# A place's mix weights issued ahead of its share of the weights' conversion, and two conversion steps moved

## The chip, the cores and the metric

The kernel runs on one core of a Trainium2 chip. A core has five engines that run side by side, each through its own instructions in order: TensorE (matrix products; PE in the profile, its weight loads PEld), VectorE (DVE), ScalarE (ACT), GpSimd (POOL) and SyncE (SP, which only issues DMAs here). They wait for each other through semaphores. The metric is the device time of one execution in microseconds (us).

## The reference

Attention with the heads mixed before and after the softmax, then a gated two-layer network without bias:

```python
# q, k, v: (8, 12, 448, 64); w_pre, w_post: (12, 12); w_in: (768, 2048); w_out: (2048, 768)
scores = np.matmul(q, k.transpose(0, 1, 3, 2)) / np.sqrt(64)
scores = np.einsum('bhij,hg->bgij', scores, w_pre)
scores = scores - np.max(scores, axis=-1, keepdims=True)
attn = np.exp(scores)
attn = attn / (np.sum(attn, axis=-1, keepdims=True) + 1e-09)
attn = np.einsum('bhij,hg->bgij', attn, w_post)
x = np.matmul(attn, v)                  # heads put side by side: (3584, 768)
h = x @ w_in
out = (h - np.tanh(h)) @ w_out          # (3584, 768), float32
```

`w_in` and `w_out` arrive as 64-bit floats. The chip computes in 32 bits, so the kernel converts them itself.

## The kernel before, in words

There are two stages. In the first (to about 848 us of the span) the kernel computes the attention, one batch after another, and beside it converts the weights. In the second it runs the network in blocks of 512 rows.

**Places.** The attention goes through 180 places, `for p in range(NPL + 3)` at L1255. One place handles two groups of ten tokens each, all twelve heads of a group lying across the partitions. The loop body gives every engine its instructions of this place, and each engine keeps the order in which they were issued (`in_order`, L134). Before the change a place `p` issues, in this order:

1. `mixed()`: ScalarE copies the result of the last mix out of PSUM (L966, or L973 in two pieces).
2. `conv.place()`: this place's share of the weights' conversion (below), in places 5 to 180.
3. SP's DMAs: `gather` brings the scores of later groups (L906), `issue(6)` sends up to six waiting loads and stores (L765).
4. `premix(p)`: TensorE multiplies the gathered scores by `w_pre` into two PSUM banks `ps_p` (L917). The pool has just these two banks, so the next premix needs both to have been read.
5. `norm(p - 1)`: VectorE adds 1e-9 to the sums `zs` of the exponentials of the place before (L937, twice) and takes the reciprocal (L938); GpSimd multiplies `w_post` by it into `wr` (L939). This folds the softmax's division into the mix weights.
6. `expo(p)`: for each of the two banks VectorE takes the maximum (L926), and ScalarE the exponential with its sum (L928).
7. Jobs planned ahead for this place: scores of a head pair (L873), transposes of q or k (L839, L813), or a half of the values (L998); and the copies that take their results out of PSUM (L878, L824, L825, L852, L854, L1016).
8. `mix(p - 1)`: TensorE multiplies the exponentials of the place before by `wr` (L956).

Places differ in length: 64 of them hold values, and the others one or two head pairs of scores or a transpose.

**The conversion.** 48 quads of four 128 x 128 blocks are converted. `Convert.place` (L50) advances every quad under way by one step a place and starts a new one when it is due, at the earliest three places after the last; at most two are in their earlier steps. `narrow_quad` (L72) is a generator with seven steps:

1. VectorE: clamp the upper word (L81), shift the lower word (L82).
2. GpSimd: scale the upper word (L84). ScalarE: scale the lower word (L85).
3. VectorE: sign (L90), join (L91), exponent (L94).
4. GpSimd: multiply and add (L96, L97); the result is `m`.
5. ScalarE: rounded copy of `m` (L100). GpSimd: four sums of the blocks (`sums_in` L112 or `sums_out` L123), which the second stage's seven-product scheme needs.
6. GpSimd: the remainder of `m` (L103). In `w_out`'s quads ScalarE flips the sign of one sum (L131). GpSimd: rounded copy of the sums, their high part (L105). A DMA of the converted words is put in the slow queue.
7. GpSimd: the remainder of the sums (L108). A DMA of the sums is put in the slow queue.

Of the kernel before, what the change touches and what calls it, by code (L numbers as in the profile page):

```python
# [11 lines left out]
F32R = mybir.dt.float32r  # L12
# [3 lines left out]
ALU = mybir.AluOpType  # L16
# [5 lines left out]
def raw(ap):  # L22

    return ap.bitcast(F32)
# [47 lines left out]
def narrow_quad(nc, pool, dma, r, dst, sums, sums_dst):  # L72

    p = r.shape[0]
    hi, lo = r[:, :, :, 1], r[:, :, :, 0]
    u, w = hi, lo


    lim = 122879.9921875
    m = pool.tile([p, 4, 128], F32, name="cm", tag="cm", bufs=2)  # L80
    nc.vector.tensor_scalar(m, hi.bitcast(F32), lim, -lim, op0=ALU.min, op1=ALU.max)  # L81
    nc.vector.tensor_scalar(w, lo, 8, None, op0=ALU.logical_shift_right)  # L82
    yield
    nc.gpsimd.tensor_scalar(m, m, 2.0**-112, None, op0=ALU.mult)  # L84
    nc.scalar.mul(w.bitcast(F32), w, 2.0**-44)  # L85
    yield
    o = pool.tile([p, 4, 2, 128], F32R, name="co", tag="co", bufs=2)
    oh, ol = o[:, :, 0], o[:, :, 1]
    s = ol.bitcast(I32)
    nc.vector.tensor_scalar(s, hi, -(2**31), None, op0=ALU.bitwise_and)  # L90
    nc.vector.scalar_tensor_tensor(  # L91
        out=u, in0=m.bitcast(I32), scalar=3, in1=s, op0=ALU.logical_shift_left, op1=ALU.bitwise_or
    )
    nc.vector.tensor_scalar(s, u, -(2**23), None, op0=ALU.bitwise_and)  # L94
    yield
    nc.gpsimd.tensor_tensor(out=m, in0=w.bitcast(F32), in1=s.bitcast(F32), op=ALU.mult)  # L96
    nc.gpsimd.tensor_tensor(out=m, in0=m, in1=u.bitcast(F32), op=ALU.add)  # L97
    yield
    t = pool.tile([p, 4, 2, 128], F32, name="ct", tag="ct", bufs=2)
    nc.scalar.copy(oh, m)  # L100
    done = sums(nc, m, t[:, :, 1])
    yield
    nc.gpsimd.tensor_sub(ol, m, raw(oh))  # L103
    done()
    nc.gpsimd.tensor_copy(t[:, :, 0].bitcast(F32R), t[:, :, 1])  # L105
    dma(dst, raw(o).rearrange("p x t n -> p x (t n)"))
    yield
    nc.gpsimd.tensor_sub(t[:, :, 1].bitcast(F32R), t[:, :, 1], t[:, :, 0])  # L108
    dma(sums_dst, t.rearrange("p s t n -> p s (t n)"))

# [40 lines left out]
def kernel_body(  # L151
# [11 lines left out]
    nc = tc.nc  # L163
# [72 lines left out]
    def open_ps_h():  # L236
        ff.ps_h = ctx.enter_context(tc.tile_pool(name="ps_h", bufs=2, space=PSUM, side="left"))
# [497 lines left out]
    with ExitStack() as st:  # L735
# [32 lines left out]
        def issue(most):  # L768
            for x in (queue, slow):
                while x and most and x[0][0] < place[0]:  # L770
                    send(x, nc.sync)
                    most -= 1
# [130 lines left out]
        def gather(t, eng=nc.sync):  # L903
            i, g = groups[t]
            x = tq[t % RT]
            eng.dma_start(x[D - HP : D - HP + rows[t], :], sts[i][tokens[t].start : tokens[t].stop : tokens[t].step])  # L906
            tg[t] = x

        def premix(p):


            pss = [ps_p.tile([P, S], F32, name="ps_p", tag="ps_p") for _ in halves]
            ts = [tg.pop(2 * p + j) for j in range(2)]
            for j in (1, 0):
                for r in (1, 0):
                    k = slice(r * D, D + r * H * half_rows(2 * p + j)[r])
                    nc.tensor.matmul(pss[r][halves[j], :], wpre[k, :], ts[j][k, :], start=True, stop=True)  # L917
            return pss

        def expo(p, pss):  # L920
            zs = gp.tile([P, 3, 2], F32, name="zs", tag="zs")
            es = []
            for r, ps in enumerate(pss):

                mx = gp.tile([P, 1], F32, name="mx", tag="mx")
                nc.vector.tensor_reduce(out=mx, in_=ps, axis=AX.X, op=ALU.max, negate=True)  # L926
                e = gp.tile([P, S], F32, name="e", tag="e", bufs=4)
                nc.scalar.activation(e, ps, AF.Exp, bias=mx, scale=1.0, accum_out=zs[:, 0, r : r + 1])  # L928
                es.append(e)
            te[p] = [es, zs]  # L930

        def norm(p):
            zs = te[p][1]
            wr = gp.tile([P, 2, D], F32, name="wr", tag="wr", bufs=2)[:, :, :HP]
            for r in range(2):

                nc.vector.tensor_scalar_add(zs[:, 1, r : r + 1], zs[:, 0, r : r + 1], 1e-9)  # L937
            nc.vector.reciprocal(zs[:, 2], zs[:, 1])  # L938
            nc.gpsimd.tensor_mul(  # L939
                wr, wpost[:, :HP].unsqueeze(1).to_broadcast([P, 2, HP]), zs[:, 2].unsqueeze(2).to_broadcast([P, 2, HP])  # L940
            )
            te[p].append(wr)

        def mix(p):

            es, _, wr = te.pop(p)
            ps = ps_o.tile([P, 2, 512], F32, name="ps_o", tag="ps_o")
            for j in range(2):
                i, g = groups[2 * p + j]
                if g == 0:  # L950
                    ats[i] = kp.tile([CP, NC, H, MT], F32, name="at", tag="at", bufs=2)
            for r, e in enumerate(es):
                for c in range(NC):
                    for j, a in enumerate(halves):
                        k = slice(a.start, a.start + H * half_rows(2 * p + j)[r])
                        nc.tensor.matmul(  # L956
                            ps[:CP, j, c * GP : (c + 1) * GP].rearrange("p (h i) -> p h i", i=GI)[:, :, r * GH : (r + 1) * GH],
                            e[k, c * CP : (c + 1) * CP], wr[k, r, :],
                            start=True, stop=True,
                        )  # L960

            def rest():
                (i0, _), (i1, _) = groups[2 * p], groups[2 * p + 1]
                n0, n1, at = rows[2 * p] // H, rows[2 * p + 1] // H, at_of[2 * p]
                if i0 == i1 and n0 == n1 == GI:
                    nc.scalar.copy(  # L966
                        ats[i0][:, :, :, at : at + 2 * GI].rearrange("p c h (j i) -> p j (c h) i", j=2),
                        ps[:CP, :, : NC * GP].rearrange("p j (x i) -> p j x i", i=GI),
                    )
                    return  # L970
                for j, (i, n) in enumerate(((i0, n0), (i1, n1))):
                    at = at_of[2 * p + j]
                    nc.scalar.copy(  # L973
                        ats[i][:, :, :, at : at + n],
                        ps[:CP, j, : NC * GP].rearrange("p (c h i) -> p c h i", c=NC, i=GI)[:, :, :, :n],
                    )

            return rest
# [161 lines left out]
        NPL = NG // 2  # L1140
# [23 lines left out]
        at_s, p, kind = {}, 0, None  # L1164
# [35 lines left out]
        for i, (b, m) in enumerate(blocks):  # L1200
            p0 = first[i] // 2
            if i + 2 < len(blocks):
                p = at_s[i + 2, 0] - 1
# [7 lines left out]
        for b in range(1, B):  # L1211
            p, o, done = first[blocks.index((b - 1, 1))] // 2 - 4, 0, []
            for hq in range(3):
                if hq == 2:

                    p = max(p, done[0] + 1)
# [38 lines left out]
        for p in range(NPL + 3):  # L1255
            if mixed:
                mixed()
                mixed = None
            if 5 <= p < NPL + 1:
                conv.place()  # L1260
            place[0] += 1
            for t in (2 * p + 4, 2 * p + 5):
                if t < NG:
                    gather(t)
            issue(6)
            if p == NPL + 1:
                for f in start.pop(p):
                    f()
            if p < NPL:
                ps = premix(p)  # L1270
            if 1 <= p < NPL + 1:
                norm(p - 1)
            if p == NPL:
                for f in x0[1:]:
                    f()
            if p < NPL:
                expo(p, ps)
            for f, *a in todo[p]:
                f(*a)
            for f in sooner:  # L1280
                f()
            sooner.clear()
            if 1 <= p < NPL + 1:
                mixed = mix(p - 1)
            for f in then + last:
                f()
            then.clear()
            last.clear()
            if p == NPL - 3:
                conv.rest(now)  # L1290
                early.close()
                open_early()
            if p == NPL - 1:
                early_ps.close()
                open_ps_h()
            for f in start.get(p, ()):
                f()
            for _ in range(pieces.get(p, 0)):
                next(xl)
# [88 lines left out]
```

## Time and profile before

| | |
|---|---|
| median of 3 runs | 1738.76 us (1728.68 to 1739.03) |
| profiled execution | 1736.07 us, span 1734.3 us |
| granted TensorE clock | 0.988 |
| busy: PE, PEld | 1670.9 us (96%), 1388.2 us (80%) |
| busy: DVE, ACT, POOL | 1233.1 us (71%), 1090.7 us (63%), 585.2 us (34%) |
| GpSimd idle ahead of L105, for ScalarE's L131 | 57.9 us |
| GpSimd idle ahead of L939, for VectorE's L938 | 186.6 us |

A line of the profile names engine, line and tile (out<-in); "idle before" is the time in which that engine did nothing ahead of the instruction, and the releaser is what ended the wait. A busy TensorE is not one at its peak, since matmuls are pipelined and their ends are modelled. The idle time of an engine costs nothing unless a later one waits for it.

### The profile page before, as it was taken

Reading aid. Unit: us, or ns where it says so; the run is one execution under the profiler, and the core shown is the slowest. Engines: PE = TensorE matmul, PEld = TensorE weight load, DVE = VectorE, ACT = ScalarE, POOL = GpSimd, SP = SyncE. Lnnn points to the kernel's source line nnn. Section 1 sums busy time; section 2 is a strip of 40 time slices with the busy share of each in tenths; the row PEclk is TensorE's granted clock in tenths of the full one; section 3 lists DMA queues with packets and bytes.
Section 4 is the critical chain, followed back from the end, with each engine's and each line's share of the span. In section 5 each row is a group of like instructions: output and inputs, shape, how many; then the busy total and the mean of one; then the engine's idle time right before and its main releaser. Section 6 shows DMA issues by size and latency. Waiting matters only on the chain.

```text
span 1734.3 us, 41218 instructions
## 1 busy us (share of the span) xinstructions
PE 1670.9 (96%) x16068; PEld 1388.2 (80%) x16068; DVE 1233.1 (71%) x2119; ACT 1090.7 (63%) x1920; POOL 585.2 (34%) x798
## 2 busy tenths in 40 slices
PE   8999999999999999999998999899998899999999
PEld 6776777777777677677787778788887788989999
DVE  5776777878777777775497999568776868788432
ACT  4766677777677777776486767356665365666331
POOL 1466567666666666661100111101101101101100
PEclk9999999999999999999999999999999999999999
DMA  8778889898987979865778889889889889988993
GB/s 177 218 222 246 249 235 276 248 267 255 257 253 234 259 248 257 256 203 163 249 267 282 293 286 332 306 272 347 317 309 369 298 261 346 302 316 328 402 414 139
DMA packets 322290, 475.09 MB, mean 274 GB/s; under 512 B 105264, under 2 KB 255280, under 8 KB 322096
## 3 DMA queue, kind: packets, MB, share of 16 engines
q1 hardware_dynamic: 305660, 414.34, 74.4%
q0 software_dynamic: 16128, 57.68, 8.7%
q8 instruction: 128, 2.10, 0.5%
q14 instruction: 66, 0.54, 0.1%
q10 hardware_dynamic: 308, 0.43, 0.1%
HBM read 274.73 MB, written 120.59 MB: 228 GB/s over the span
## 4 chain that ended last, share of the span: by engine, by line
PE 67%; DVE 10%; DMA 8%; issue 5%; ACT 5%; POOL 4%; SPq 1%; DVEq 0%; ACTq 0%; POOLq 0%
PE ps_o L956 11%; PE ps_m L998 6%; PE ps_p L917 6%; PE ps_h L290 6%; PE y L533 6%; PE y L531 6%; PE ps_h L291 6%; PE y L532 6%; PE ps_h L293 6%; PE ps_q L873 4%; DMA t<-s 2%; DMA vr<-in_v_dram 1%; ACT e L928 1%; DVE qa L319 1%; DMA gl<-gs 1%
## 5 line engine op out<-in xcount | busy, mean ns | idle before, releaser
L956 PEld LDWEIGHTS ps_o<-wr,e 60*112 60x112 f32 (+1 forms) x5760 | 304.6, 175 | 46.2 <-POOL wr L939 31.8
L956 PE MATMUL ps_o<-wr,e 60*112 60x60 f32 (+1 forms) x5760 | 315.6, 259 | 16.5 <-POOL wr L939 15.3
L928 ACT ACTIVATE e<-ps_p,mx 128x448 f32<-128x448 f32 x360 | 224.7, 630 | 115.1 <-DVE mx L926 83.1
L926 DVE TENSOR_REDUCE mx<-ps_p 128x1 f32<-128x448 f32 x360 | 206.5, 615 | 108.3 <-PE ps_p L917 107.7
L966 ACT COPY at<-ps_o 112x960 f32<-112x960 f32 x156 | 154.4, 989 | 109.1 <-PE ps_o L956 108.7
L917 PE MATMUL ps_p<-t,wpre 60*64 60x448 f32 (+1 forms) x1440 | 182.6, 571 | 5.9 <-DMA t<-s 5.7
L998 PEld LDWEIGHTS ps_m<-at,vr 112*64 112x64 f32 x3072 | 150.0, 138 | 26.6 <-ACT at L973 8.6
L998 PE MATMUL ps_m<-at,vr 112*64 112x120 f32 (+1 forms) x3072 | 164.2, 264 | 2.9 <-DMA vr<-in_v_dram 2.8
L531 PE MATMUL y<-w,gh 128*128 128x384 f32 x448 | 152.5, 340 | 8.0 <-DMA w<-ts 5.6
L533 PE MATMUL y<-w,gl 128*128 128x384 f32 x424 | 144.7, 341 | 7.3 <-DVE gl L449 7.3
L939 POOL TENSOR_TENSOR wr<-wpost,zs 128x120 f32<-128x120 f32 x180 | 70.0, 389 | 241.9 <-DVE zs L938 186.6
L532 PE MATMUL y<-w,gh 128*128 128x384 f32 x448 | 151.4, 338 | 0.0
L873 PEld LDWEIGHTS ps_q<-kk,qh 64*120 64x120 f32 (+1 forms) x768 | 58.8, 173 | 82.1 <-issue 45.8
L873 PE MATMUL ps_q<-kk,qh 64*120 64x448 f32 (+1 forms) x768 | 121.3, 392 | 1.1 <-DVE kk L825 0.5
L878 DVE COPY s<-ps_q 120x448 f32<-120x448 f32 (+1 forms) x192 | 112.1, 614 | 7.8 <-PE ps_q L873 7.4
L668 POOL DMA_DIRECT2D gs<-gb x24 | 17.2, 717 | 297.6 <-DVE gb L667 282.0
L306 ACT ACTIVATE u<-h 128x1024 f32<-128x1024 f32 x56 | 59.5, 1062 | 76.3 <-DVE h L715 71.1
L878 ACT COPY s<-ps_q 120x448 f32<-120x448 f32 (+1 forms) x192 | 94.9, 537 | 6.9 <-PE ps_q L873 6.7
L443 ACT CAST gh<-gl 128x1024 fp32r<-128x1024 f32 x61 | 63.5, 1042 | 53.8 <-DMA gl<-gs 20.9
L531 PEld LDWEIGHTS y<-w,gh 128*128 128x128 f32 x448 | 85.1, 190 | 13.6 <-ACT u L306 3.4
L646 POOL DMA_DIRECT2D gs<-ga x24 | 17.2, 717 | 224.1 <-DVE ga L329 224.1
L532 PEld LDWEIGHTS y<-w,gh 128*128 128x128 f32 x448 | 85.1, 190 | 3.4
(372 smaller groups left out, 3995.3 us busy)
## 6 DMA issues: line engine op xcount, KB each, us to landing
t<-s SPq DMA_DIRECT2D x342, 210.0 KB
wa<-ss SPq DMA_DIRECT2D x96, 384.0 KB
w<-wo SPq DMA_DIRECT2D x43, 768.0 KB
gl<-gs SPq DMA_DIRECT2D x62, 512.0 KB
wa<-wi SPq DMA_DIRECT2D x72, 384.0 KB
w<-ts SPq DMA_DIRECT2D x35, 768.0 KB
gs<-gs POOLq DMA_DIRECT2D x24, 768.0 KB, 9.7
cr<-in_moe_w_in_dram SPq DMA_DIRECT2D x48, 256.0 KB
```

The source lines that it names most:

```text
L290: nc.tensor.matmul(ph, w[:, c, 0], xh, start=start and c == 0, stop=False, skip_group_check=True)
L531: nc.tensor.matmul(y, gh[:, tok], wh, start=first, stop=False, skip_group_check=True)
L532: nc.tensor.matmul(y, gh[:, tok], wl, start=False, stop=False, skip_group_check=True)
L533: nc.tensor.matmul(y, gl[:, tok], wh, start=False, stop=last, skip_group_check=True)
L873: nc.tensor.matmul(ps[:n, :S], qx[a, hp, :], kx[a, hp % 2], start=(x == 0), stop=(x == 2))
L878: eng(sts[i][:n, 2 * hp + j, :], ps[:n, :S])
L917: nc.tensor.matmul(pss[r][halves[j], :], wpre[k, :], ts[j][k, :], start=True, stop=True)
L926: nc.vector.tensor_reduce(out=mx, in_=ps, axis=AX.X, op=ALU.max, negate=True)
L928: nc.scalar.activation(e, ps, AF.Exp, bias=mx, scale=1.0, accum_out=zs[:, 0, r : r + 1])
L956: nc.tensor.matmul(ps[:CP, j, c * GP : (c + 1) * GP].rearrange("p (h i) -> p h i", i=GI)[:, :, r * GH : (r + 1) * GH], e[k, c * CP : (c + ...
L966: nc.scalar.copy(ats[i0][:, :, :, at : at + 2 * GI].rearrange("p c h (j i) -> p j (c h) i", j=2), ps[:CP, :, : NC * GP].rearrange("p j (x ...
L998: nc.tensor.matmul(pv[j * D : (j + 1) * D, r, :n], vt[:, j, c, :], ats[i][:, c, 2 * hp + j, :n], start=(c == 0), stop=(c == NC - 1),)
```

## The change

Three edits. `norm(p - 1)` moves from behind `premix(p)` to the front of `conv.place()`, so in each place its two adds, reciprocal and product stand ahead of that place's conversion instructions on VectorE and GpSimd. In step 2 the scaling of the upper word goes from GpSimd to ScalarE, ahead of the scaling of the lower word there. GpSimd's rounded copy of the sums goes from step 6 to step 7.

```diff
@@ narrow_quad
     yield
-    nc.gpsimd.tensor_scalar(m, m, 2.0**-112, None, op0=ALU.mult)
+    nc.scalar.mul(m, m, 2.0**-112)
     nc.scalar.mul(w.bitcast(F32), w, 2.0**-44)
     yield
...
     nc.gpsimd.tensor_sub(ol, m, raw(oh))
     done()
-    nc.gpsimd.tensor_copy(t[:, :, 0].bitcast(F32R), t[:, :, 1])
     dma(dst, raw(o).rearrange("p x t n -> p x (t n)"))
     yield
+    nc.gpsimd.tensor_copy(t[:, :, 0].bitcast(F32R), t[:, :, 1])
     nc.gpsimd.tensor_sub(t[:, :, 1].bitcast(F32R), t[:, :, 1], t[:, :, 0])
     dma(sums_dst, t.rearrange("p s t n -> p s (t n)"))
@@ kernel_body, the loop over places
             if mixed:
                 mixed()
                 mixed = None
+            if 1 <= p < NPL + 1:
+                norm(p - 1)
             if 5 <= p < NPL + 1:
                 conv.place()
...
             if p < NPL:
                 ps = premix(p)
-            if 1 <= p < NPL + 1:
-                norm(p - 1)
```

## The prediction

> **What bounds the kernel now.** I read the page's first lines for the whole, then two stretches of the first stage (180 places; the conversion of the weights runs beside them from place 5 until about 780 us), then the waits inside that stretch.
>
> ```profile
> span 1734.3 us, 41218 instructions
> PE 1670.9 (96%) x16068; PEld 1388.2 (80%) x16068; DVE 1233.1 (71%) x2119; ACT 1090.7 (63%) x1920; POOL 585.2 (34%) x798
> 50.00:790.00 740.00, 718.53 (x10480) 551.48 (x10480) 548.02 (x1378) 526.54 (x1207) 485.11 (x616) 0.99 0.83 246
> 790.00:850.00 60.00, 58.13 (x875) 45.37 (x871) 31.43 (x88) 38.91 (x88) 6.61 (x18) 0.98 0.53 185
> ```
>
> TensorE is the bound: in the stretch with the conversion it is busy 718.5 of 740 us, at a granted clock of 0.99. So the change can win at most the 21.5 us that are left, and a little that hides inside stretched work. GpSimd falls from 485 us of 740 to 6.6 of 60 when the conversion ends: its load there is the conversion. Who makes TensorE wait in that stretch:
>
> ```profile
> POOL ct L105 <- ACT ct L131: 57.9, 22, 4.4
> PEld ps_o L956 <- POOL wr L939: 27.4, 37, 2.1
> PE ps_o L956 <- POOL wr L939: 13.9, 17, 1.7
> ```
>
> The columns are total us, times, longest. TensorE waits for the mix weights `wr`: its weight loads 27.4 us in 37 places, its matmuls 13.9 us in 17 of these (in the others the array was still streaming). GpSimd itself stands 57.9 us in front of L105 for ScalarE's sign flip, with `wr` queued behind. That is what this change is aimed at.
>
> **The change part by part.** The seven steps of one conversion fall into seven places in a row, and the next one starts about three places later, so there are three kinds of places: 1-4-7 (VectorE L81, L82; GpSimd L96, L97, L108), 2-5 (L84, L85, the sums, ScalarE's L100) and 3-6 (VectorE L90, L91, L94; GpSimd L103, L105). One pair of neighbours, a 2-5 place and the 3-6 place after it, shows the loop that sets TensorE's pace beside its own work:
>
> ```profile
> 208.79 0.98 PE L917 MATMUL ps_p<-t,wpre 60*64 60x448 f32 x8
> 208.91 0.98 ACT L966 COPY at<-ps_o 112x960 f32<-112x960 f32 x1
> 209.79 0.61 ACT L100 CAST co<-cm 128x512 fp32r<-128x512 f32 x1
> 210.31 0.67 ACT L85 ACTIVATE cr<-cr 128x512 f32<-128x512 int32 x1
> 210.88 0.62 ACT L928 ACTIVATE e<-ps_p,mx 128x448 f32<-128x448 f32 x1
> 212.00 0.20 ACT L928 ACTIVATION_READ_ACCUMULATOR e<-ps_p,mx 128x1 f32 x1
> 212.96 0.98 PE L917 MATMUL ps_p<-t,wpre 60*64 60x448 f32 x8
> 213.72 0.42 DVE L90 TENSOR_SCALAR co<-cr 128x512 int32<-128x512 int32 x1
> 213.87 0.67 PE L873 MATMUL ps_q<-kk,qh 64*120 64x448 f32 x4
> 214.24 0.69 DVE L91 SCALAR_TENSOR_TENSOR cr<-cm,co 128x512 int32<-128x512 int32 x1
> 214.97 0.43 DVE L94 TENSOR_SCALAR co<-cr 128x512 int32<-128x512 int32 x1
> 215.31 0.21 DVE L937 TENSOR_SCALAR zs<-zs 128x1 f32<-128x1 f32 x2
> 215.64 1.13 DVE L926 TENSOR_REDUCE mx<-ps_p 128x1 f32<-128x448 f32 x2
> 215.87 0.39 POOL L939 TENSOR_TENSOR wr<-wpost,zs 128x120 f32<-128x120 f32 x1 [3.54 <-DVE zs L938]
> 216.31 1.78 PE L956 MATMUL ps_o<-wr,e 60*112 60x60 f32 x32 [1.56 <-POOL wr L939]
> 217.47 0.20 ACT L928 ACTIVATION_READ_ACCUMULATOR e<-ps_p,mx 128x1 f32 x1
> 218.02 0.98 PE L917 MATMUL ps_p<-t,wpre 60*64 60x448 f32 x8
> ```
>
> (Each row: start, us, engine, line; in brackets the idle time before it and what ended it.) The exponentials end at 212.20 and 217.67; `wr` could be made at once, but its sums stand behind L90 to L94 on VectorE, so the mix starts only at 216.31. The next premix (L917) needs the two `ps_p` banks, so it comes after both exponentials. From premix to the end of the exponentials, the loop takes 3.41 us in the first place and 4.71 in the second.
>
> *Norm in front.* It removes nothing from any engine; it moves two adds, a reciprocal and L939 ahead of the conversion. `wr` is then ready 0.33 (215.31 to 215.64) + 0.15 (gap to L939) + 0.39 = some 0.9 us after the exponentials, 1.6 us or more before the mix wants it in nearly all places. A gap of the weight loads hides about 0.1 us each under the stream (estimate: they run that far ahead), so the gain is 27.4 - 37 x 0.1 = 23.7 us, between the rows' 13.9 and 27.4. But the conversion now stands behind a wait for the exponentials, on VectorE and on GpSimd. Queued behind it on VectorE are L81/L82 or L90/L91/L94 and then the maxima, for which the next exponentials wait; on GpSimd the rest of the conversion. No DMA is moved past a queue: the gathers and the loads on SP keep their places.
>
> *3-6 places.* Until now GpSimd was done with L103 before VectorE came to L90; now both start together, behind the same reciprocal. Above, L90 to L94 ran alone; what company costs them, these rows show (602.39 is one of the few executions of L94 that had it):
>
> ```profile
> 601.25 0.54 POOL L939 TENSOR_TENSOR wr<-wpost,zs 128x120 f32<-128x120 f32 x1
> 601.66 0.69 DVE L91 SCALAR_TENSOR_TENSOR cr<-cm,co 128x512 int32<-128x512 int32 x1
> 601.76 1.72 POOL L108 TENSOR_TENSOR ct<-ct 128x512 fp32r<-128x512 f32 x1
> 602.39 1.37 DVE L94 TENSOR_SCALAR co<-cr 128x512 int32<-128x512 int32 x1
> L103 POOL TENSOR_TENSOR co<-cm,co x48: 1267/1280/1292, 71.9 to 776.6; 128x512 fp32r<-128x512 f32 x48
> L94 DVE TENSOR_SCALAR co<-cr x48: 426/427/1380, 61.7 to 766.9; 128x512 int32<-128x512 int32 x48
> 217.44 1.48 POOL L96 TENSOR_TENSOR cm<-cr,co 128x512 f32<-128x512 f32 x1
> 217.68 1.52 DVE L82 TENSOR_SCALAR cr<-cr 128x512 int32<-128x512 int32 x1
> ```
>
> L91 to the end of L94 took 2.10 us beside L108, against 1.16 us alone (214.24 to 215.40); L82 beside L96 shows the same, ending 0.28 us after its partner. L103 has L108's form (1.28 us in both medians), so I take the whole extra 0.94 us (bounds 0 and 0.94). By the Trainium skill, SBUF — State Buffer, Who interferes with whom, VectorE and GpSimd share a pair of ports, the first holds it for its whole instruction, and the other blocks fully; L108 would then last 1.28 + 0.59 = 1.87 us, the row has 1.72, and the sum would rise by 31 x 0.15, about 4 us. After the exponentials, a 3-6 place now needs 0.33 (norm) + 1.59 + 0.94 (conversion) + 2.03 (215.64 to 217.67, maxima and exponentials) = 4.89 us.
>
> *How long a place is.* TensorE alone takes about 3.86 us for premix, two head pairs' scores and mix; 0.65 less with one pair (the 0.67 of L873); 2 us more with values:
>
> ```profile
> 270.03 0.98 PE L917 MATMUL ps_p<-t,wpre 60*64 60x448 f32 x8
> 273.89 0.61 PE L917 MATMUL ps_p<-t,wpre 60*64 60x448 f32 x4
> L998 PEld LDWEIGHTS ps_m<-at,vr x3072: 132/137/231, 52.9 to 859.7; 112*64 112x64 f32 x192
> ```
>
> 3072 / 48 = 64 of 180 places have values and hide all of this. Of 48 conversions 48 x 116 / 180 = 31 meet a short place. Behind a short 2-5 place the exponentials end as the 3-6 place begins: 4.89 - 3.86 = 1.0 us lost. Behind a long one they end earlier, and VectorE's copies of the values (to 0.6 us before, estimate) start the sum: 4.89 - 0.6 - 3.86 = 0.45. Half of each: 31 x 0.73 = 23 us lost. Without the extra 0.94 it is 16 x 0.1, say 2 to 5 us.
>
> *1-4-7 places.* L82 loses its long partner (L96 and L97 come later now): the loop is shorter there, and worth nothing more than the wait already counted.
>
> *Upper word on ScalarE.* 48 instructions of L84's 1.49 us leave GpSimd; that is off TensorE's path once `wr` runs first. ScalarE gets 48 more like L85.
>
> ```profile
> L84 POOL TENSOR_SCALAR cm<-cm x48: 1486/1490/1505, 53.4 to 762.2; 128x512 f32<-128x512 f32 x48
> L85 ACT ACTIVATE cr<-cr x48: 658/677/746, 58.2 to 763.9; 128x512 f32<-128x512 int32 x48
> L105 POOL CAST ct<-ct x48: 602/611/807, 73.2 to 779.6; 128x512 fp32r<-128x512 f32 x48
> L108 POOL TENSOR_TENSOR ct<-ct x48: 1264/1275/1722, 75.8 to 780.5; 128x512 fp32r<-128x512 f32 x48
> L97 POOL TENSOR_TENSOR cm<-cm,cr x48: 1281/1293/1507, 64.3 to 771.4; 128x512 f32<-128x512 f32 x48
> ```
>
> From L85 to the next instruction 0.57 us pass (210.31 to 210.88), and there ScalarE waits for nothing: the loop of a 2-5 place grows from 3.41 to 3.98 us. Against 3.86 that is 0.12 us, in a place of 3.2 us up to 0.8; about a third of the 31 are longer or split the two ScalarE jobs over two places. I take 20 x 0.45 = 9 us (bounds 2 and 13). The Trainium skill, ScalarE: Activation LUTs, Rules for kernel authors, puts a multiplication on VectorE and budgets about 0.3 us + 0.83 ns an element, 0.73 us here; by it the sum would be 3 us higher.
>
> *The sums' high part.* L105 (0.61 us) goes from a 3-6 to a 1-4-7 place, and GpSimd's 57.9 us for L131 go with it; what they cost TensorE is inside the 23.7. Its DMA was issued after L108 in the same place and still is.
>
> Sum: -23.7 + 23 + 9 = +8 us. The profiled execution took 1736.07 us, 1.8 more than its span, so **1744 us**. The median of the three runs, 1738.76, lies 2.7 us above it; they spread 0.6%, and about 1% is what a measurement can tell from no change.
>
> **The rivals.**
>
> *No collision* (0.25): GpSimd's L103 starts late enough, or gives way, so L94 keeps its 0.43 us. For it: L94's median here is 0.427 us, so most executions ran alone. Against: both are released by one reciprocal now. -23.7 + 4 + 9 = -11: 1725 us.
>
> *All hidden* (0.06): the two loops never reach TensorE's length, because it waits for other things in the same places (DMAs). The whole 23.7 us stay: 1712 us. Against: the pair above has 0.76 us between the exponentials and the next premix, and less in shorter places.
>
> *ScalarE waits for GpSimd* (0.18; the slower side): in a 1-4-7 place GpSimd now starts behind the reciprocal and has `wr` 0.39, L105 0.61, L108 1.28, L96 and L97 1.3 each: 0.48 + 4.9 = 5.3 us after the exponentials. ScalarE comes to L100, which reads L97's result, 1.0 us into the next place (208.79 to 209.79). It decides from the point where the place plus what the exponentials ended ahead of it is under 4.35 us; then L100 holds the exponentials behind it. Up to 0.7 us in each of 31 short places on top of the sum: +22, 1766 us. Against: a short place often has a long one ahead, which gives 2 us.
>
> *The change doesn't do what it says*: `wr` is early, but TensorE waits at the premix instead of at the mix. It is part of the forecast (in the second place above only 0.35 us of the 1.56 can be won).
>
> **How the numbers follow.** Forecast 0.51, rivals 0.25, 0.06, 0.18. The range takes the forecast's bounds (23.7 down to 14 gained, 13 us on ScalarE) and reaches into the rivals on both sides: 1722 to 1760. More than 1% faster (under 1719) is the hidden case and a bit of the collision-free one: 0.07. More than 1% slower (over 1753) is most of the waiting case and the forecast's upper bounds: 0.18. The rest, 0.75, is within 1%.
>
> **What would show it.** The wait of L956 for L939 should fall from 27.4 us to under 3, GpSimd's for L131 to nothing, L84's line should be ScalarE's with about 0.65 us. In 3-6 places L94 should take over 1 us in most executions, and L917 should wait for L928, or premix to premix be over 4.5 us in short places. L100 waiting for L97 would show the slow rival. I am wrong if L94 stays near 0.43 us, or if TensorE's busy time in the stretch stays 718 us in a clearly shorter one.

## The result, and the profile after

The changed kernel takes 1781.17 us (median of 4 runs, 1775.97 to 1786.9) against 1736.37 us of before: a ratio of 1.0266, interval 1.0217 to 1.0315. It is slower by 45 us, and outside the predicted range of 1722 to 1760. The profiled execution has a span of 1774.3 us, 40.0 more than before.

L84 is ScalarE's now, and the sums' high part has become L107 (the former L105); the other lines keep their numbers. (In some experiments lines stand up to 12 further down; the text then gives the number of before too.) First the head of the page, and the busy time of the stretch in which the conversion now runs (us, instructions; the columns are PE, PEld, DVE, ACT, POOL, granted clock, DMA share, GB/s). Its last L103 starts 45 us later than in before (821.9 against 776.6).

```profile
span 1774.3 us, 41193 instructions
PE 1701.3 (96%) x16068; PEld 1400.9 (79%) x16068; DVE 1249.6 (70%) x2119; ACT 1114.6 (63%) x1968; POOL 546.3 (31%) x750
50.00:830.00 780.00, 747.66 (x10414) 563.88 (x10412) 561.65 (x1368) 548.30 (x1251) 445.83 (x567) 0.98 0.78 232
```

TensorE executes the same 16068 matmuls as before and is busy 30 us longer. Waits inside a group of matmuls are mostly counted as busy time, and a slower clock stretches the group as well: the premix takes 0.98 us in the prediction's rows, below 1.59 at 102.32, where its second bank comes late, and 2.38 at 108.74, at half the clock. The waits in 50 to 830 us say where (total us, times, longest):

```profile
ACT e L928 <- DVE mx L926: 129.5, 103, 3.7
PEld ps_p L917 <- ACT e L928: 33.0, 66, 1.7
PEld ps_o L956 <- POOL wr L939: 16.4, 23, 2.0
ACT co L100 <- POOL cm L97: 15.1, 16, 1.7
PE ps_p L917 <- ACT e L928: 12.4, 22, 1.5
PE ps_o L956 <- POOL wr L939: 7.9, 12, 1.6
```

The wait of the mix for `wr` has gone from 27.4 to 16.4 us, not to under 3. In its place, the premix L917 waits for the exponentials L928, 33.0 us of its weight loads (0.3 us in before). And ScalarE's L100 waits for GpSimd's L97 in 16 places (in before it never did). The two lines that were to collide, in the view of their lines (min, median, max in ns):

```profile
L94 DVE TENSOR_SCALAR co<-cr x48: 428/1380/1403, 61.3 to 808.6; 128x512 int32<-128x512 int32 x48
L103 POOL TENSOR_TENSOR co<-cm,co x48: 1269/1717/1738, 74.9 to 821.9; 128x512 fp32r<-128x512 f32 x48
```

Both medians rose, from 427 and 1280 ns. How these meet is seen in the timeline of a 1-4-7 place's GpSimd work, the 2-5 place behind it and the 3-6 place that follows (rows in between are left out):

```profile
98.61 1.29 POOL L97 TENSOR_TENSOR cm<-cm,cr 128x512 f32<-128x512 f32 x1
...
99.94 0.62 ACT L100 CAST co<-cm 128x512 fp32r<-128x512 f32 x1 [0.76 <-POOL cm L97]
100.30 1.65 PEld L956 LDWEIGHTS ps_o<-wr,e 60*112 60x112 f32 x32 [0.51 <-POOL wr L939]
100.47 0.62 ACT L84 ACTIVATE cm<-cm 128x512 f32<-128x512 f32 x1
101.00 0.66 ACT L85 ACTIVATE cr<-cr 128x512 f32<-128x512 int32 x1
101.56 0.61 ACT L928 ACTIVATE e<-ps_p,mx 128x448 f32<-128x448 f32 x1
102.17 0.62 ACT L928 ACTIVATE e<-ps_p,mx 128x448 f32<-128x448 f32 x1
102.32 1.59 PE L917 MATMUL ps_p<-t,wpre 60*64 60x448 f32 x8 [0.23 <-ACT e L928]
102.69 0.19 ACT L928 ACTIVATION_READ_ACCUMULATOR e<-ps_p,mx 128x1 f32 x1
102.78 0.95 ACT L824 CAST kk<-ps_m 128x448 fp32r<-128x448 f32 x2
103.33 1.16 DVE L825 TENSOR_TENSOR kk<-ps_m,kk 128x448 fp32r<-128x448 f32 x2 [2.45 <-ACT kk L824]
104.41 0.20 DVE L937 TENSOR_SCALAR zs<-zs 128x1 f32<-128x1 f32 x2
104.96 0.42 POOL L939 TENSOR_TENSOR wr<-wpost,zs 128x120 f32<-128x120 f32 x1 [2.92 <-PE ps_q L873]
105.17 0.76 DVE L91 SCALAR_TENSOR_TENSOR cr<-cm,co 128x512 int32<-128x512 int32 x1
105.34 1.71 POOL L103 TENSOR_TENSOR co<-cm,co 128x512 fp32r<-128x512 f32 x1
105.43 1.78 PE L956 MATMUL ps_o<-wr,e 60*112 60x60 f32 x32 [0.48 <-POOL wr L939]
105.96 1.37 DVE L94 TENSOR_SCALAR co<-cr 128x512 int32<-128x512 int32 x1
107.26 1.14 DVE L926 TENSOR_REDUCE mx<-ps_p 128x1 f32<-128x448 f32 x2
107.96 0.63 ACT L928 ACTIVATE e<-ps_p,mx 128x448 f32<-128x448 f32 x1 [2.91 <-DVE mx L926]
108.59 0.62 ACT L928 ACTIVATE e<-ps_p,mx 128x448 f32<-128x448 f32 x1
108.74 2.38 PE L917 MATMUL ps_p<-t,wpre 60*64 60x448 f32 x8 [1.52 <-ACT e L928]
109.10 0.20 ACT L928 ACTIVATION_READ_ACCUMULATOR e<-ps_p,mx 128x1 f32 x1
```

Read it as a chain. GpSimd began the 1-4-7 place behind the reciprocal (its L939 starts at 94.71, then come L107, L108 and L96), so L97 ends only at 99.90. L100 waits 0.76 us for it and has L84 and L85 behind it, so the exponentials end at 102.88. ScalarE's copies L824 then come late, VectorE's L825 too, and the sums L937 behind them: `wr` is late although it stands in front of the conversion, and the mix waits. Now L90, L91 and L94 run between the sums and the maxima, L94 beside L103, and the next exponentials end only at 109.30. The premix waits 1.52 us. One late exponential made the next one later.

What follows that wait is the granted clock (same columns as above):

```profile
104.30:107.70 3.40, 2.43 (x38) 1.91 (x35) 3.30 (x8) 0.76 (x1) 2.09 (x2) 1.00 0.77 240
107.75:114.50 6.75, 5.76 (x34) 3.70 (x34) 4.10 (x13) 4.93 (x12) 4.51 (x5) 0.50 0.57 197
602.60:606.00 3.40, 1.87 (x22) 0.89 (x20) 3.37 (x9) 2.01 (x6) 0.52 (x2) 1.00 0.94 239
606.10:609.40 3.30, 3.13 (x31) 2.69 (x30) 1.68 (x4) 2.35 (x7) 3.22 (x4) 0.50 1.03 275
```

From 107.7 on TensorE has half its clock for 6.8 us, and from 606.1 for 3.4. The trace holds 8 such stretches between places 5 and 179, 34.1 us together; that of before holds 4, 13.7 us. Half of the difference, 10.2 us, is my estimate of what they cost: it is the loss if all of TensorE's work there takes twice as long and none of it hides a wait.

**Where the 40 us are.** I summed, over places 5 to 179, the time from the start of each group of TensorE's matmuls to the start of the next, and took out of each the half of the time at clock 0.50 (the estimate above, the column "clock"). Groups that begin or end at a premix (L917) show the waits for exponentials and gathers; those that end at a mix (L956) the waits for `wr`; "stage" is the sum. In before the premix groups hold 457.5 us, the mix groups 294.3, other 40.0, the clock 6.8: 798.7. The difference to before, in us, one profiled execution each:

| kernel | median, before on the same chip | premix | mix | other | clock | stage |
|---|---|---|---|---|---|---|
| changed kernel | 1781.2, 1736.4 | +38.9 | -4.9 | 0.0 | +10.2 | +44.3 |
| e1 norm | 1763.4, 1733.8 | +33.3 | -11.5 | +0.1 | 0.0 | +21.9 |
| e2 ScalarE | 1739.2, 1733.8 | +6.0 | -1.8 | +0.1 | +1.7 | +6.0 |
| e3 sums | 1734.4, 1733.8 | +1.2 | -3.9 | +0.1 | -3.4 | -6.0 |
| e4 norm, sums | 1767.1, 1733.8 | +32.6 | -7.2 | +0.3 | +8.5 | +34.2 |
| e5 norm on VectorE | 1748.9, 1733.4 | +15.7 | -7.5 | -0.2 | +8.5 | +16.6 |
| e6 norm on GpSimd | 1759.0, 1733.4 | +1.4 | +8.4 | +0.1 | +13.7 | +23.6 |
| e7 norm, ScalarE | 1769.3, 1733.4 | +40.4 | -10.2 | +0.1 | +5.1 | +35.4 |
| e8 all, norm on GpSimd | 1761.6, 1733.4 | +12.2 | +2.5 | +0.1 | +6.8 | +21.6 |
| e9 ScalarE, sums | 1738.1, 1736.7 | +5.3 | -2.5 | +0.1 | +3.4 | +6.2 |
| e10 all, L103 ahead | 1749.3, 1736.7 | +23.1 | -7.7 | +0.1 | +5.1 | +20.6 |
| e11 all, step 4 first | 1794.9, 1736.7 | +41.2 | -2.9 | +2.9 | +23.9 | +65.0 |
| e12 all, old order in 3-6 | 1755.3, 1736.7 | +12.1 | -1.4 | +0.1 | +6.8 | +17.6 |
| e13 e10 without ScalarE | 1760.1, 1735.1 | +23.4 | +0.3 | -0.1 | +5.1 | +28.7 |
| e14 all, behind maxima | 1761.1, 1735.1 | +4.2 | +6.2 | +3.4 | +18.8 | +32.7 |
| e15 e14 without ScalarE | 1752.1, 1735.1 | +4.1 | +0.6 | +1.9 | +3.4 | +10.1 |
| e16 all, ScalarE's share late | 1745.6, 1738.8 | +13.2 | -4.8 | +1.9 | -3.4 | +6.9 |
| e17 e16, norm behind | 1771.5, 1738.8 | -3.3 | +25.8 | +1.7 | +13.7 | +37.9 |
| e18 e10, L84, L85 late | 1744.3, 1738.8 | +12.5 | -8.8 | +2.0 | +5.1 | +10.8 |

Executions of one kernel differ by half a per cent, so a profiled stage and a median can differ by some 9 us; the columns say in which form the time is lost.

### The profile page after: what moved, and what is told of

It is laid out like the page before. It is cut to its first block, busy times and chain, and to the rows that moved or that the text cites. A ratio compares the mean times of both kernels' runs of the same rounds, so it can differ in the third digit from the quotient of the medians.

```text
span 1774.3 us, 41193 instructions
## 1 busy us (share of the span) xinstructions
PE 1701.3 (96%) x16068; PEld 1400.9 (79%) x16068; DVE 1249.6 (70%) x2119; ACT 1114.6 (63%) x1968; POOL 546.3 (31%) x750
## 4 chain that ended last, share of the span: by engine, by line
PE 60%; DVE 12%; DMA 9%; ACT 8%; POOL 5%; issue 5%; SPq 1%; ACTq 0%; DVEq 0%; POOLq 0%
PE ps_o L956 7%; PE ps_h L290 6%; PE ps_h L291 6%; PE ps_h L293 6%; PE ps_p L917 6%; PE y L533 5%; PE y L531 5%; PE y L532 5%; PE ps_m L998 5%; ACT e L928 4%; PE ps_q L873 3%; DMA t<-s 3%; DVE mx L926 1%; DVE co L94 1%; POOL ct L108 1%
## 5 line engine op out<-in xcount | busy, mean ns | idle before, releaser
L956 PEld LDWEIGHTS ps_o<-wr,e 60*112 60x112 f32 (+1 forms) x5760 | 306.4, 176 | 36.5 <-POOL wr L939 21.0
L956 PE MATMUL ps_o<-wr,e 60*112 60x60 f32 (+1 forms) x5760 | 315.2, 259 | 10.2 <-POOL wr L939 9.3
L928 ACT ACTIVATE e<-ps_p,mx 128x448 f32<-128x448 f32 x360 | 224.3, 629 | 148.4 <-DVE mx L926 146.4
L917 PE MATMUL ps_p<-t,wpre 64*64 64x448 f32 (+1 forms) x1440 | 209.1, 578 | 20.8 <-ACT e L928 12.4
L939 POOL TENSOR_TENSOR wr<-wpost,zs 128x120 f32<-128x120 f32 x180 | 75.8, 421 | 411.3 <-DVE zs L938 338.8
L873 PE MATMUL ps_q<-kk,qh 64*120 64x448 f32 (+1 forms) x768 | 127.1, 404 | 1.2 <-DVE kk L825 0.5
L878 DVE COPY s<-ps_q 120x448 f32<-120x448 f32 (+1 forms) x192 | 112.4, 613 | 10.1 <-PE ps_q L873 10.0
L443 ACT CAST gh<-gl 128x1024 fp32r<-128x1024 f32 x61 | 63.5, 1041 | 53.7 <-DMA gl<-gs 18.8
L531 PEld LDWEIGHTS y<-w,gh 128*128 128x128 f32 x448 | 85.3, 190 | 12.5 <-ACT qa L307 5.2
L917 PEld LDWEIGHTS ps_p<-t,wpre 64*64 64x64 f32 (+1 forms) x1440 | 48.6, 133 | 51.2 <-ACT e L928 34.0
L533 PEld LDWEIGHTS y<-w,gl 128*128 128x128 f32 x424 | 80.7, 190 | 9.3 <-DVE gl L449 9.3
```

Of the source, the lines that this page charges most:

```text
L531: nc.tensor.matmul(y, gh[:, tok], wh, start=first, stop=False, skip_group_check=True)
L533: nc.tensor.matmul(y, gl[:, tok], wh, start=False, stop=last, skip_group_check=True)
L873: nc.tensor.matmul(ps[:n, :S], qx[a, hp, :], kx[a, hp % 2], start=(x == 0), stop=(x == 2))
L878: eng(sts[i][:n, 2 * hp + j, :], ps[:n, :S])
L956: nc.tensor.matmul(ps[:CP, j, c * GP : (c + 1) * GP].rearrange("p (h i) -> p h i", i=GI)[:, :, r * GH : (r + 1) * GH], e[k, c * CP : (c + ...
```

## The experiments

**The three parts, alone and in pairs.** Theory A: the order of the work (the norm in front) is the cause. Theory B: it is ScalarE's extra work. Each of these kernels is the one before with one or two of the change's three edits.

```diff
 e1:  +norm(p - 1) in front of conv.place(), -norm(p - 1) behind premix(p)
 e2:  -nc.gpsimd.tensor_scalar(m, m, 2.0**-112, None, op0=ALU.mult)   +nc.scalar.mul(m, m, 2.0**-112)
 e3:  the sums' nc.gpsimd.tensor_copy moved behind the yield
 e4:  e1 and e3      e7:  e1 and e2      e9:  e2 and e3
```

> Only the first edit: the mix weights in front of the conversion; the upper word's scaling stays on GpSimd (1.49 us, L84) and the sums' high part in step 6. Theory A (the order is the cause: VectorE's and GpSimd's conversion both start behind the exponentials, collide, and the premix then waits): this alone costs most of the 45 us, +25 to +40 us against before, L94 near 1.37 us, L917 waiting for L928 for over 20 us. Theory B (ScalarE's extra 48 instructions are the cause): within 10 us of before, or faster.

> Only the second edit: the upper word scaled on ScalarE. Theory A: the loop of a 2-5 place grows by 0.57 us and GpSimd loses 71 us of work that stood ahead of the mix weights: between -8 and +8 us against before. Theory B: +25 to +40 us, premix waiting for the exponentials in 2-5 places.

> Only the third edit: the sums' high part a step later. GpSimd no longer waits 57.9 us for the sign flip, and TensorE's waits for the mix weights behind L105 and L84 (about 9 us of weight loads) should shrink. Both theories: -3 to -10 us against before.

> First and third edit, without ScalarE's. Theory A: about e1 less some us, +20 to +40. Theory B: faster than before by 5 to 15 us. Against the changed kernel (+45 us) it tells what ScalarE's edit adds when the order is changed: by A under 15 us, by B nearly all.

> Norm in front and the upper word on ScalarE, the sums' high part where it was. If the parts add up: 1763 + 5 = 1768 us. If ScalarE's extra 0.57 us hits only where the new order has made the 2-5 place the tight one (chains from 2-5 to 3-6 places): 1775 to 1785 us, that is the whole of the changed kernel.

> The upper word on ScalarE and the sums' high part later, the norm behind the conversion as before. If the three parts add up: 1739 + 1 = 1740 us or a little less (GpSimd's 72 us wait for L131 is gone). If ScalarE's extra 0.57 us is what costs in company of the later high part, as the changed kernel's 14 us over norm and sums suggest: 1750 us or more.

Measured, as ratios: e1 1.0161 (1.0120 to 1.0203), e2 1.0025 (1.0005 to 1.0046), e3 0.9998 (0.9978 to 1.0018), e4 1.0191 (1.0159 to 1.0223), e7 1.0197 (1.0178 to 1.0217), e9 1.0010 (0.9995 to 1.0026). In medians: the norm alone +30 us, ScalarE +5, the sums +1. Both theories had expected the sums alone to be 3 to 10 us faster; they do nothing to the time, so GpSimd's wait for L131 was off the path. Theory A holds: the norm in front carries two thirds of the 45 us. Added up the three give 36, as e7 (1769, where 1768 was expected from adding up) and e9 bear out for pairs. The changed kernel is 9 us above that sum; with intervals of 7 to 9 us either way on e1 and on the changed kernel, it isn't shown that all three together cost more than the parts. In e1 (waits, 50 to 830 us) the wait did what the fourth rival said, it moved:

```profile
PEld ps_p L917 <- ACT e L928: 30.8, 54, 1.7
PEld ps_o L956 <- POOL wr L939: 9.0, 17, 1.1
```

**Which engine's order.** The norm has a half on VectorE (L937, L938) and one on GpSimd (L939). In e5 only the first is in front, in e6 only the second; e8 is e6 with the other two parts. In e6 and e8 the lines of `narrow_quad` and below stand 6 further down.

```diff
 e5 (on e1):
-                norm(p - 1)
+                weights = norm(p - 1)      # adds and reciprocal; L939 is returned
             if 5 <= p < NPL + 1:
                 conv.place()
+            if 1 <= p < NPL + 1:
+                weights()
 e6 (on e1), e8 (on the changed kernel): in Convert.place, steps 1 and 3 first, then the norm, then the rest
+        for x in vec:
+            next(x, None)
+        between()                          # norm(p - 1)
+        for x in rest:
+            next(x, None)
```

> Norm alone in front, but of its two halves only VectorE's (two adds, reciprocal): GpSimd's L939 (L940 here) goes back behind the conversion's GpSimd work. Theory 'order on VectorE': the 1.5 us of L90 to L94 still stand between the exponentials and the maxima, so most of the cost of the norm in front (1763 against 1734) stays, and the mix waits for wr again: 1750 to 1770 us. Theory 'collision alone': L103 no longer starts with the reciprocal, L94 falls from 1.37 to about 0.43 us in most executions and the time to 1735 to 1742 us.

> Norm alone, in front only on GpSimd: on VectorE the conversion's L81/L82 or L90/L91/L94 come first and the sums after them, as before; on GpSimd L939 comes in front of the conversion's work. Theory 'order on VectorE' and theory 'collision': L94 is back near 0.43 us, the waits of L917 for L928 fall from 30.8 to under 5 us and the time is that of before or a little less, 1720 to 1738 us. If the order on GpSimd is what costs (L100 behind L97, L103 late), it stays above 1755 us.

> The whole change, but on VectorE the conversion comes first and the sums after it, as before (GpSimd's order stays the changed one). Theory 'order on VectorE': 1725 to 1742 us, L917 waits under 10 us for L928 (45 in the changed kernel). If the order on GpSimd costs, above 1765 us.

Measured: e5 1.0076 (1.0053 to 1.0098), e6 1.0133 (1.0112 to 1.0155), e8 1.0165 (1.0137 to 1.0193). e5, 1748.9 us, lies just under the range of "order on VectorE" (1750 to 1770) and above that of "collision alone" (to 1742): half of e1's loss stays. L94 did not come free of company there (mean 796 ns; in 18 places it now meets L108). For e6 and e8 I was wrong. With VectorE's old order the premix hardly waits for the exponentials any more (its weight loads 1.1 us in e6, 7.6 in e8), but the time is lost elsewhere. In e6 the mix waits longer (+8.4 us) and the clock takes 13.7 us more than in before. In e8 the premix column is still the largest, +12.2, with waits for gathers and for ScalarE's copies of the mix (L973, there L979) in it, and the clock takes 6.8. One new cause is in the lines of e6: L91 (there L97) waits for L84 (L90), which now stands behind L939 on GpSimd,

```profile
L97 DVE SCALAR_TENSOR_TENSOR cr<-cm,co 128x512 int32<-128x512 int32 x48 | 33.3, 694 | 27.6 <-POOL cm L90 24.2 <-DVE co L96 0.5
```

24.2 us of VectorE's time in front of the sums. So VectorE's old order alone is no remedy: in e6, with the conversion first there, the mix waits, and in e1, with the norm first, the premix.

**The collision, and the 3-6 places.** e10 puts L103 ahead of the norm, so that it runs before the exponentials end; e12 leaves the whole norm behind the conversion in the 48 places of the third step.

```diff
 e10 (on the changed kernel): in Convert.place, step 6 first, then the norm, then the rest
 e12 (on the changed kernel):
+            behind = 5 <= p < NPL + 1 and [x for x in conv.active if x[1] == 2]
-            if 1 <= p < NPL + 1:
+            if 1 <= p < NPL + 1 and not behind:
                 norm(p - 1)
             if 5 <= p < NPL + 1:
                 conv.place()
+            if behind:
+                norm(p - 1)
```

> The changed kernel, but in 3-6 places GpSimd does L103 ahead of the norm, so that it runs before the exponentials end and not beside L91 and L94. Theory 'collision': L94 is back at 0.43 us in most of 48 executions (1.38 now), the loop after the exponentials falls from 4.9 to about 3.95 us, the waits of L917 for L928 from 45 to under 25 us, the time from 1781 to about 1750 to 1760 us. Theory 'order on VectorE' (the 1.6 us of L90 to L94 inside the loop suffice): L94 falls, the time stays above 1772 us.

> The changed kernel, but in the 48 places of the third step (L90, L91, L94) the norm stays behind the conversion; in all others it is in front. If the 3-6 places carry the loss and start the chains: L917's waits for L928 fall from 45 to under 10 us and the time to 1730 to 1745 us, near before or below. If the order in the 1-4-7 and 2-5 places carries it as well: above 1760 us.

e10: 1749.29 us, 1.0070 (1.0046 to 1.0095). Moving one GpSimd instruction gives back 32 of the 45 us. In the view of its lines L94 (there L100, mean 494 ns) is short again in 37 of 48 places, and the premix's wait (waits, 50 to 830 us) is halved:

```profile
L100 DVE TENSOR_SCALAR co<-cr 128x512 int32<-128x512 int32 x48 | 23.7, 494 | 1.7
L109 POOL TENSOR_TENSOR co<-cm,co 128x512 fp32r<-128x512 f32 x48 | 61.3, 1278 | 0.4 <-ACT co L106 0.2
```

```profile
PEld ps_p L923 <- ACT e L934: 15.6, 39, 0.7
PEld ps_o L962 <- POOL wr L945: 9.8, 15, 1.5
```

The longest wait fell from 1.7 to 0.7 us. From the end of one place's exponentials to the end of the next, 27 of the 48 3-6 places of the changed kernel take 4.9 us, and 26 of e10's take 3.9 to 4.0, the 3.95 that was expected. So taking the collision away gives back most of the loss. e5, in which L94 doesn't meet L103 either, is 15 us above before, much as e10 is 13 above, which points at VectorE's order for that rest. e12 came out between its two cases: 1755.34 us, 1.0098 (1.0062 to 1.0134). The old order in the 3-6 places alone gives back some 26 us of the 45. Such shares don't add up, since each of these edits breaks the same chain at another link (e16 below gives back 38 with the collision half in place).

**L100 behind L97.** In 1-4-7 places e11 has GpSimd do L96 and L97 before L107 and L108.

```diff
 e11 (on the changed kernel):
-        for x in list(self.active):
+        for x in sorted(self.active, key=lambda x: x[1] == 6):
             next(x[0], None)
```

> The changed kernel, but in 1-4-7 places GpSimd does L96 and L97 before the high part and L108 of the older conversion, so L97 ends 1.9 us earlier. Theory 'ScalarE waits for GpSimd, and that starts the chains': L100's waits for L97 fall from 15.1 to under 3 us and the time by 15 to 25 us, to 1757 to 1766. If those waits only lie beside others: within 6 us of 1781.

It came out 14 us above the changed kernel, their intervals just overlapping: 1794.88 us, 1.0346 (1.0302 to 1.0390). L100's wait for L97 is gone, as meant, and neither case that I had written down covers the outcome. TensorE's waits in 50 to 830 us, then SP's:

```profile
PEld ps_p L917 <- ACT e L928: 20.9, 44, 1.7
PE ps_p L917 <- DMA t<-s: 15.6, 12, 3.6
```

```profile
SPq L765 <- POOL wr L939: 130.0, 29, 8.2
SPq L765 <- POOL co L103: 37.0, 17, 5.8
SPq L765 <- POOL ct L108: 22.6, 11, 4.6
```

L108 is last on GpSimd now, up to the next place's L939. The store of its sums (L765) stands in SP's queue and waits for it; the gathers (L906) of the next place stand behind that store, and the premix waits 15.6 us for them (4.0 in before). The first SP row names L939, but these stores go out as L108 ends (at 99.96, for one, with L108 over at 99.93 and L939 running until 100.28), so that wait is for L108. The premix column is no better than the changed kernel's (+41.2 against +38.9), and the clock takes 23.9 us more than in before, against 10.2. The changed kernel has the same wait in small: SP waits for L108 and L103 169 us, against 28 before (17.9 and 10.1),

```profile
SPq L765 <- POOL ct L108: 98.9, 41, 5.2
SPq L765 <- POOL co L103: 70.4, 34, 4.6
```

but the gathers still came in time there (6.1 us of premix waits).

**What e10 still loses.** e13 is e10 with L84 back on GpSimd. e14 puts the whole share of the conversion behind the maxima and exponentials; e15 is e14 with L84 on GpSimd. e16 to e18 issue ScalarE's steps behind the exponentials and the copies of the scores, where ScalarE waits for the next maxima.

```diff
 e14 (on the changed kernel), e15 (on e4):
-            if 5 <= p < NPL + 1:
-                conv.place()
...
             if p < NPL:
                 expo(p, ps)
+            if 5 <= p < NPL + 1:
+                conv.place()
 e16 (on the changed kernel: steps 2, 5), e17 (on e9: steps 2, 5), e18 (on e10: step 2):
             sooner.clear()
+            conv.late()                    # the steps that place() has set aside
```

> The norm in front, the sums' high part later, L103 ahead of the norm in 3-6 places, the upper word on GpSimd as before. If what e10 lost (13 us over before) is ScalarE's extra 0.57 us in 2-5 places: 1730 to 1740 us. If it is VectorE's 1.6 us of conversion in the loop: 1745 to 1752 us, as e10.

> The changed kernel, but a place's whole conversion share stands behind the maxima and exponentials on every queue instead of in front of them. If the loss is VectorE's conversion between the exponentials and the maxima: L917's waits for L928 fall from 45 to under 10 us and the time to 1720 to 1738 us. If the loss goes with the collisions or GpSimd's lateness wherever the work stands (L100 behind L97, copies of the scores late): 1750 us or more.

> As e14, with the upper word on GpSimd as before. If ScalarE's extra work costs wherever it stands: 5 to 10 us under e14. If it costs only in the loop: within 4 us of e14.

> The changed kernel, but the 2-5 places' share of the conversion (L84, L85, then L100 and GpSimd's sums) is issued behind the place's exponentials and score copies, so ScalarE does it while it waits for the next maxima. L103 then starts only some 1.9 us into the 3-6 place, after L94. If ScalarE's 1.9 us ahead of the exponentials and the collision are the loss: L94 back near 0.43 us, L917's waits for L928 from 45 to under 15 us, 1725 to 1745 us. If VectorE's order alone suffices for the loss: above 1755 us.

> As e16 with the norm behind the conversion, as before. ScalarE's part no longer costs in the loop (5 us of L917's waits in e9), but L103 waits for L100 in front of the norm and wr comes later: 1730 to 1750 us; under 1728 us if only the loop counted.

> As e10 (L103 ahead of the norm), with ScalarE's L84 and L85 alone behind the exponentials and score copies. If ScalarE's 1.25 us ahead of the exponentials in the 2-5 places are what e10 still loses: 1730 to 1742 us against its 1749. If not: 1745 or more.

e13 missed both cases: 1760.13 us, 1.0140 (1.0102 to 1.0178), 12 us slower than e10 (each against its own before). So L84 on ScalarE gains once L103 runs ahead, while alone it costs 5 us (e2). With L84's 1.49 us on GpSimd, L103 (L109) ends late, and L939 (L945) stands behind it: in the places with a wait, it is what ended last ahead of L945 in 12.9 of the 22.7 us. The mix waits, the premix does not wait longer than in e10:

```profile
PEld ps_o L962 <- POOL wr L945: 22.7, 31, 1.7
PEld ps_p L923 <- ACT e L934: 13.0, 37, 0.7
```

e14 (1.0131, 1.0082 to 1.0180) and e15 (1.0099, 1.0072 to 1.0126) take away the premix's wait for exponentials altogether (the 4 us left in the table are gathers and copies), but are slower than before. The mix waits about as long as in before (23.7 us of weight loads in e14). By what ended last ahead of L939, 13.4 of these belong to VectorE's copies of scores, of k and of values, which now come late and hold the sums, and 10.3 to L97 on GpSimd. In e14's profiled execution, the slowest of its four, the clock takes the most, 18.8 us. With ScalarE's extra step e14 is 9 us above e15; their intervals overlap, so that price isn't clear of noise. By time e14 falls into its second case and e15 into its first.

e16: 1745.56 us, 1.0048 (1.0017 to 1.0079), just over the range that was expected. e18: 1744.27 us, 1.0045 (1.0019 to 1.0071), between its two cases, 5 us below e10. With ScalarE's steps behind the exponentials 38 of the 45 us are back in e16, even though L94 (there L103) still meets company in half of its places:

```profile
L103 DVE TENSOR_SCALAR co<-cr 128x512 int32<-128x512 int32 x48 | 40.7, 848 | 1.6
```

e17 has the same late ScalarE steps and the norm behind the conversion, and takes 1771.45 us, 1.0215 (1.0162 to 1.0268); I had expected at most 1750. L103 then stands in front of `wr` and waits for L100 (144 us in 48 places), as the expectation had said, but at a higher price:

```profile
PEld ps_o L965 <- POOL wr L948: 55.8, 52, 2.6
```

So with late ScalarE steps the norm in front is worth 26 us (e17 to e16), and with early ones it costs 43 (e9 to the changed kernel). No kernel here is faster than the one before.

## Why the prediction was wrong

The forecast was +8 us in the sum; the profiled stage shows +44.3. By its own terms:

- **The loss in 3-6 and 2-5 places: right in kind and nearly in size.** Predicted 23 + 9 = 32 us, measured 38.9 in the premix column. Of the two terms the norm's was too small (33.3 in e1) and ScalarE's too large (6.0 in e2, 7.1 from e1 to e7). The collision is there: L94 1.38 us (1.37 predicted) and L103 1.72. In the chain above the exponentials end at 102.88 and 109.30, 6.42 us apart. In the pair of places 108 and 109, which has no late copies in it, the timeline shows the loop by itself:

```profile
550.90 0.21 ACT L928 ACTIVATION_READ_ACCUMULATOR e<-ps_p,mx 128x1 f32 x1
...
552.65 1.40 DVE L94 TENSOR_SCALAR co<-cr 128x512 int32<-128x512 int32 x1
...
555.81 0.20 ACT L928 ACTIVATION_READ_ACCUMULATOR e<-ps_p,mx 128x1 f32 x1
```

  The exponentials end at 551.11 and 556.01: 4.90 us, where 4.89 was worked out. The 2-5 place of that pair has its premix at 547.18, so its loop is 3.93, predicted 3.98. What the sum missed is that a late end of one place is the late start of the next: it priced a 2-5 and a 3-6 place one by one. (A slip of 0.02 us, 4.89 - 0.6 - 3.86 being 0.43 and not 0.45, changes nothing.)
- **The gain: the step that failed.** "The wait of L956 for L939 should fall from 27.4 us to under 3": it fell to 16.4, and the mix column gained 4.9 us instead of 23.7. The working asked when `wr` is ready after the exponentials (0.9 us), and took the end of the exponentials as it was in before. But the same change moved that end, by up to 1.7 us (the premix's longest wait), and what follows the exponentials on ScalarE and VectorE with it. By what ended last ahead of L939 in the places with a wait, 9.2 us belong to L97, still in front of L939 on GpSimd from the place before, 3.6 to L825 and 3.6 to L1016, copies that VectorE makes in front of the sums. Where less of the wait is left the gain is larger: 11.5 us in e1, 8.8 in e18.
  The price was too high as well. No run shows the 0.1 us that a gap was taken to hide: 27.4 us of weight loads against 13.9 of matmuls is 0.36 us a gap. In before, the mix groups with such a wait are together 18.9 us longer than the median of groups behind the same work without one, and 13.3 in the changed kernel. That difference, 5.6 us, is what the mix column shows, and 23.7 was not there to be won.
- **The clock: left out.** 10.2 us by the estimate above, more than a quarter of the 36 us by which the stage missed. The rows of before had the clock at 0.99 for the stretch, and I read the mean, not its dips.
- **The slow rival (0.18)** came true in 16 places, not in 31: L100 waited 15.1 us for L97, 0.94 each. Its price of 22 us was counted on top of independent places, and no run shows it by itself. In e4 L100 waits as much (14.1 us, against 5.0 in e1), and e4 is 4 us above e1, within the intervals. That taking the wait away helps was not shown: e11 took it away and had SP's queue to pay for.
- **No collision (0.25), predicted 1725:** it did not come true; L94 had company in 46 of 48 places. e10 made the case nearly pure and gave 1749. Both of the other terms of its sum were off there as well: 7.7 us gained instead of 23.7, 23.1 lost at the premix instead of 13, and 5.1 of clock.
- **ScalarE's L84** took 0.632 us (about 0.65 predicted) and cost 5 us alone (bounds 2 and 13). The **sums' high part** was rightly given nothing. "No DMA is moved past a queue" was true of the order and not enough: the stores became ready later, and SP stood 169 us for them.

By the Trainium skill, SBUF — State Buffer, Who interferes with whom, L103 should have been blocked for the rest of the L91 that it met, 1.87 us in all as the prediction estimated for L108. Its median is 1.72, as L108's row of before had it. The two differ by 0.15 us a place, 31 x 0.15 = 4.7 us in the prediction's sum, and the measured value decides.

What stays open: why some stretches are followed by a slow clock and others, with as much idle time, are not; what a fall really costs, since the column is an estimate; and whether the 9 us by which the changed kernel exceeds the sum of its parts are real.

## What to carry to other kernels

When an instruction is moved in front of others in an in-order queue, work out the new time of what it waits for, not only its own: here the exponentials moved with it, and the gain counted from their old end was not there. Price neighbouring steps of a loop as a chain, longest loop first, and ask which instruction of another engine becomes free at the same event: here one reciprocal released VectorE and GpSimd together, and putting one GpSimd instruction ahead of it gave back 32 of the 45 us. A short wait of TensorE can cost more than its length: in these traces the clock often fell behind it.

## What the runs showed of the hardware

The granted clock fell to 0.50 in stretches of 3.41 us and multiples, always on one grid of 3.41 us, and after waits much shorter than that. I cut the first stage of all 20 traces into the stretches of that grid at full clock and counted in each the time without a matmul. Of some 4300 stretches with less than 0.6 us idle none was followed by a slow one; of 192 with 0.6 to 1.0 us 15 were, of 56 with 1.0 to 1.2 us 20, of 35 with 1.4 to 1.6 us 24, of 44 with more 34. One fall at half the clock for 3.41 us costs up to 1.7 us (an estimate, as above), as much as the wait that came before it. In the stretch from 602.60 to 606.00 above TensorE is busy 1.87 of 3.40 us, idle for 1.53 in sum, and the clock falls. The Trainium skill, TensorE: Matmul & The Clock Gate, HAM oscillation, gives as its rule no idle gaps over about 3.4 us; these traces have falls after much less. No kernel here tested the cause by itself; it is read from the traces.

What company costs depends on which instruction was there first. L94 alone takes 0.43 us. Wherever it began while GpSimd's L103 or L108 ran and was the last of the two to end (175 executions in the 20 traces), it ended 0.28 to 0.29 us after GpSimd's instruction: above, L103 ends at 107.05 and L94 at 107.33. So the length of L94 is set by what is left of the other one. The 0.44 us that L103 takes longer in the changed kernel belong to L91 and not to L94. Where L103 or L108 began with 0.08 us of L91 still to run, it took 1.28 us although L94 followed beside it (2 executions); with 0.47 us to run 1.60 (12), and with 0.58 to 0.60 us 1.72 (226).
